# Moving an 18 KB weight load from SyncE's queue to ScalarE's queue in a grouped 1x1 convolution

## The chip, the cores and the metric

The kernel runs on 1 core of one Trainium2 chip. The metric is the device time of one execution in microseconds (us), lower is better. Each run also has a span, from the first to the last instruction or transfer that the profiler records; it is some 2 us shorter than the time.

## The reference

```
x: (1, 512, 512, 192) bf16      w: (1, 1, 4, 48, 48) bf16
xg  = x.reshape(1, 512, 512, 4, 48)
out = einsum('bhwgc,gcd->bhwgd', xg, w[0, 0])     # k = 1, no padding
```

Each of 262,144 pixels has 192 channels in 4 groups of 48, and each group is multiplied by its own 48x48 matrix. The input and the output are 100.7 MB each; the weights are 18 KB.

## The kernel before

Pixels are cut into pieces. The input loads go out of SyncE's queue into a ring of 5 slots in SBUF (104 pixels a partition each). TensorE (PE) transposes a pair of pixel groups against an identity, VectorE (DVE) copies the transposes out of PSUM, PE multiplies with the weights, ScalarE (ACT) writes the result back into the same ring columns, and the stores go out of ScalarE's queue. The first slot is cut into pieces of 8, 20, 32 (and then whole slots of 104) so that PE can start early.

The weights come in as `w_sb`, 48 partitions with four rows of 96 bytes each. PE spreads them with a selection matrix `esel` to blocks in PSUM, and DVE copies those to `wt`, which the product matmuls read. On PE this building of the weights stands ahead of the first transposes.

```
        @block.sync
        def _(sp):
            wq = Waiter(sp)
            sp.dma_start(w_sb[:], wv).then_inc(w_sem, 16)
            for p in pieces:
                for q in pieces:
                    if q.slot == p.slot - RCOLS // BIG:
                        wq.wait(st_sem[q.i], st_val[q])        # the slot's stores have landed
                for dram, sbuf in transfers(xf, ring, p):
                    sp.dma_start(sbuf, dram).then_inc(ld_sem[p.i], 16)

        # tensor (cut)
            build_weights()                # waits for e_sem (esel) and w_sem (w_sb)
            wq.wait(id_sem, 1)
            transposes(0)                  # waits for ld_sem of the first piece
            wq.wait(wc_sem, 1)             # wt copied by DVE
            for pair in range(NP):
                if pair + 1 < NP:
                    transposes(pair + 1)
                matmuls(pair)

        @block.scalar
        def _(act):
            wq = Waiter(act)
            todo = list(stores)
            # ... (cut) per group: wait for mm_done, act.copy of o_ps into the ring, then its stores
```

## Time and profile before

| | before |
|---|---|
| time, median of 3 runs | 485.05 us (484.9 to 485.07) |
| span of the profiled run | 483.3 us |
| busy PE / ACT / DVE | 89% / 81% / 52% |
| DMA, mean over the span | 418 GB/s |
| packet time of the two big DMA queues over 16 engines | 470.8 us |

The first view is the page's row of 40 equal slices: the mean busy share of the 16 DMA engines in tenths (9 is 90% or more), and what they moved.

```profile
DMA  8999999999999999999999999999999999999993
GB/s 351 431 406 421 449 425 421 422 424 442 434 428 419 425 420 439 425 434 424 431 434 437 424 431 428 432 431 426 434 428 428 430 424 422 439 416 427 429 390 156
```

The engines are full in every slice but the first and the last. Next, stretches of the span: length, busy time of each engine, granted PE clock, DMA share and GB/s (the last two numbers).

```profile
1.00:2.00 1.00, 0.00 (x0) 0.00 (x0) 0.00 (x0) 1.00 (x1) 0.91 (x4) 1.00 0.10 10
2.00:3.00 1.00, 0.34 (x9) 0.37 (x10) 0.00 (x0) 0.08 (x1) 0.00 (x0) 1.00 0.62 110
3.00:4.00 1.00, 0.22 (x6) 0.08 (x3) 0.66 (x1) 0.00 (x0) 0.00 (x0) 1.00 1.03 370
60.00:455.00 395.00, 376.00 (x5527) 341.70 (x5526) 220.75 (x231) 345.63 (x461) 0.00 (x0) 0.99 1.00 429
...
474.00:476.00 2.00, 0.00 (x0) 0.00 (x0) 0.00 (x0) 0.00 (x0) 0.00 (x0) 0.50 0.58 244
478.00:480.00 2.00, 0.00 (x0) 0.00 (x0) 0.00 (x0) 0.00 (x0) 0.00 (x0) 0.50 0.16 66
```

The middle runs at a share of 1.00; the first 3 us and the last 15 us do not. In the tail only stores are left, and at 478 us a share of 0.16 means that two or three of the 16 engines still work. So the time is the start of the stream, plus a full stream, plus the lag of the last engine.

The start in the timeline (start, length, engine, line, operation; SPq and ACTq are the issues on SyncE's and ScalarE's queues):

```profile
0.80 1.28 ACT L260 ACT_TABLE_LOAD   x1 [0.80 <-PEq L280]
0.80 0.38 SPq L169 DMA_DIRECT2D w_sb<-in_w_dram  x1
...
1.24 3.47 SPq L175 DMA_DIRECT2D ring<-in_x_dram  x7
...
2.66 0.56 PE L188 MATMUL o_ps<-w_sb,esel 48*128 48x48 bf16 x10 [2.66 <-DMA w_sb<-in_w_dram]
...
4.68 1.44 PE L203 MATMUL xT_ps<-ident,ring 128*128 128x128 bf16 x12 [1.47 <-DMA ring<-in_x_dram]
...
7.02 1.44 PE L203 MATMUL xT_ps<-ident,ring 128*128 128x128 bf16 x12 [0.89 <-DMA ring<-in_x_dram]
```

The weight issue takes SyncE's queue from 0.80 to 1.24 us, and the seven input loads that need no ring space follow. The weights land early (PE starts on them at 2.66 us), and PE waits for each of the first input loads.

The chain of waits, followed back from the last instruction, has one long piece at its start:

```profile
2.65 21.79 DMA ring<-in_x_dram
```

Until 24.4 us the chain is a load that PE waits for, not PE's own work. After that it runs mostly through PE; its summary by line:

```profile
by line: PE o_ps L218 31.5%; PE xT_ps L203 22.2%; DMA ring<-in_x_dram 20.3%; DMA out_dram<-ring 18.9%; ACT ring L260 1.2%; issue 0.8%; SPq L175 0.3%; ACTq L254 0.2%; SPq L169 0.1%
```

So PE (54% of the chain) is a rival to the DMA engines (39%) for what sets the pace.

### The profile page before, as it was taken

To read this page: it belongs to the slowest core of one execution; us is meant where nothing else is said; L and a number is where in the kernel's file an instruction comes from. 1 tells how busy PE (TensorE), PEld (TensorE's weight loads), DVE (VectorE), ACT (ScalarE), POOL (GpSimd) and SP (SyncE) were. 2 spreads that over 40 slices of the span, in tenths; PEclk is the share of its full clock that TensorE was granted. 3 is DMA by queue.
4 is the path that set the end of the run, shared out by engine and by line. 5 is a ranking of instruction groups with operands and counts; after the bars stand their busy time and mean duration, and the time that the engine had idled before them with its cause. 6 is when DMAs were issued, how large, how long until landed. Compare 5 with 4: busy or idle time off the path is not lost.

```text
span 483.3 us, 13933 instructions
## 1 busy us (share of the span) xinstructions
PE 431.3 (89%) x6262; PEld 392.1 (81%) x6262; DVE 250.2 (52%) x262; ACT 392.6 (81%) x522; POOL 1.3 (0%) x8
## 2 busy tenths in 40 slices
PE   5699999999999999998599999979998999999910
PEld 5599888898898889887588988969787898899800
DVE  2345655656555565564256555544554655556500
ACT  2669999999999999998299999877888999999920
POOL 1000000000000000000000000000000000000000
PEclk9979999999999999999799999998999999999965
DMA  8999999999999999999999999999999999999993
GB/s 351 431 406 421 449 425 421 422 424 442 434 428 419 425 420 439 425 434 424 431 434 437 424 431 428 432 431 426 434 428 428 430 424 422 439 416 427 429 390 156
DMA packets 7834, 202.23 MB, mean 418 GB/s; under 512 B 1056, under 2 KB 1056, under 8 KB 1696
## 3 DMA queue, kind: packets, MB, share of 16 engines
q10 hardware_dynamic: 4360, 100.67, 48.7%
q1 hardware_dynamic: 3416, 100.68, 48.7%
q8 instruction: 50, 0.82, 0.6%
q14 instruction: 8, 0.07, 0.0%
HBM read 100.68 MB, written 100.66 MB: 417 GB/s over the span
## 4 chain that ended last, share of the span: by engine, by line
PE 54%; DMA 39%; ACT 1%; issue 1%; SPq 0%; ACTq 0%
PE o_ps L218 31%; PE xT_ps L203 22%; DMA ring<-in_x_dram 20%; DMA out_dram<-ring 19%; ACT ring L260 1%; SPq L175 0%; ACTq L254 0%; SPq L169 0%
## 5 line engine op out<-in xcount | busy, mean ns | idle before, releaser
L260 ACT CAST ring<-o_ps 128x768 bf16<-128x768 f32 x521 | 391.3, 802 | 68.5 <-PE o_ps L218 61.0
L242 DVE COPY xT_sb<-xT_ps 128x1536 bf16<-128x1536 bf16 (+1 forms) x261 | 249.6, 956 | 206.0 <-PE xT_ps L203 206.0
L218 PE MATMUL o_ps<-wt,xT_sb 128*128 128x144 bf16 (+1 forms) x3126 | 292.0, 236 | 5.9 <-ACT ring L260 1.3
L218 PEld LDWEIGHTS o_ps<-wt,xT_sb 128*128 128x128 bf16 x3126 | 212.0, 99 | 43.4 <-ACT ring L260 30.2
L203 PE MATMUL xT_ps<-ident,ring 128*128 128x128 bf16 x3126 | 222.7, 221 | 21.1 <-DMA ring<-in_x_dram 21.1
L203 PEld LDWEIGHTS xT_ps<-ident,ring 128*128 128x128 bf16 x3126 | 191.1, 99 | 22.7 <-DMA ring<-in_x_dram 19.8
L188 PE MATMUL o_ps<-w_sb,esel 48*128 48x48 bf16 x10 | 0.6, 210 | 2.7 <-DMA w_sb<-in_w_dram 2.7
L188 PEld LDWEIGHTS o_ps<-w_sb,esel 48*128 48x128 bf16 x10 | 0.5, 113 | 2.6 <-POOL esel L158 2.6
L236 DVE CAST wt<-o_ps 128x480 bf16<-128x480 f32 x1 | 0.7, 658 | 3.3 <-PE o_ps L188 3.3
L260 ACT ACT_TABLE_LOAD x1 | 1.3, 1283 | 0.8 <-PEq L280 0.8
L158 POOL TENSOR_SCALAR_AFFINE_SELECT esel<-esel 48x272 bf16<-48x272 bf16 x1 | 0.4, 405 | 0.0
L155 POOL MEMSET esel<- 48x272 bf16 x1 | 0.3, 318 | 0.3 <-POOLq L280 0.3
L162 POOL TENSOR_SCALAR_AFFINE_SELECT ident<-ident 128x128 bf16<-128x128 bf16 x1 | 0.3, 285 | 0.0
L156 POOL MEMSET ident<- 128x128 bf16 x1 | 0.2, 198 | 0.0
L280 POOL MEMSET const-bfloat16-1.0<- 128x1 bf16 x1 | 0.1, 102 | 0.0
L280 POOL MEMSET const-uint8-127<- 128x1 uint8 x1 | 0.1, 102 | 0.0
L280 POOL MEMSET const-float32-0.0<- 128x1 f32 x1 | 0.1, 98 | 0.3 <-issue 0.3
L280 POOL MEMSET const-float32-1.0<- 128x1 f32 x1 | 0.1, 98 | 0.0
## 6 DMA issues: line engine op xcount, KB each, us to landing
ring<-in_x_dram SPq DMA_DIRECT2D x19, 4992.0 KB, 37.5
out_dram<-ring ACTq DMA_DIRECT2D x13, 4992.0 KB, 45.5
out_dram<-ring ACTq DMA_DIRECT2D x10, 2496.0 KB, 47.7
out_dram<-ring ACTq DMA_DIRECT2D x3, 1536.0 KB, 19.7
ring<-in_x_dram SPq DMA_DIRECT2D x1, 1536.0 KB, 8.4
out_dram<-ring ACTq DMA_DIRECT2D x1, 1152.0 KB, 16.6
ring<-in_x_dram SPq DMA_DIRECT2D x1, 960.0 KB, 5.2
out_dram<-ring ACTq DMA_DIRECT2D x1, 960.0 KB, 28.6
```

Of the source, the lines that this page charges most:

```text
L155: gp.memset(esel[:], 1.0).then_inc(p0_sem, 1)
L156: gp.memset(ident[:], 1.0).then_inc(p1_sem, 1)
L158: gp.affine_select(out=esel[:], in_=esel[:], pattern=[[-1, ECOLS]], compare_op=AluOpType.is_equal, fill=0.0, base=ESHIFT, channel_multipli ...
L162: gp.affine_select(out=ident[:], in_=ident[:], pattern=[[-1, 128]], compare_op=AluOpType.is_equal, fill=0.0, base=0, channel_multiplier=1) ...
L188: last = pe.matmul(o_ps[:, NOB - 1, col:col + CG], lhsT=esel[:, s0:s0 + 128], rhs=w_sb[:, g, :], start=True, stop=True, skip_group_check=True)
L203: last = pe.transpose(xT_ps[:, g % NXP, j * 128:(j + 1) * 128], xg[:, j * 128:(j + 1) * 128], ident[:])
L218: last = pe.matmul(o_ps[:, v % NOB, c0_:c1_], lhsT=xs[:, j * 128:(j + 1) * 128], rhs=wt[:, WOFF[tc]:WOFF[tc] + (c1_ - c0_)], start=(tc == ...
L236: dve.tensor_copy(wt[:], o_ps[:, NOB - 1, 0:WCOLS]).then_inc(wc_sem, 1)
L242: dve.tensor_copy(xT_sb[pair % NXS][:, 0:n * 2 * UC].rearrange("p (g c) -> p g c", g=n), xT_ps[:, b0:b0 + n, 0:2 * UC]).then_inc(e_done, 1)
L260: act.copy(dst, o_ps[:, v % NOB:v % NOB + 2, 0:UC]).then_inc(fa_done, 1)
L280: nc = _bacc.Bacc("TRN2", target_bir_lowering=False, num_devices=1)
```

## The change

Its intent: the first instruction of SyncE's queue should be the first input load, so that the long stream of loads starts one issue time earlier. ACT has nothing to do then but its table load.

```diff
         @block.sync
         def _(sp):
             wq = Waiter(sp)
-            sp.dma_start(w_sb[:], wv).then_inc(w_sem, 16)
             for p in pieces:
@@
         @block.scalar
         def _(act):
             wq = Waiter(act)
+            act.dma_start(w_sb[:], wv).then_inc(w_sem, 16)
             todo = list(stores)
```

## The prediction

> **What bounds the kernel now.** The DMA engines. The page's slice row reads 9 tenths or more in all slices but the first and the last, 418 GB/s mean, and the stretch view has a share of 1.00 from 20 to 400 us. Summed from the packet records, the two big queues hold 470.8 us of work for each of the 16 engines, in a span of 483.3 us. PE (89%) and ACT (81%) are near, but PE stands idle 21 us for loads. Unused are the head (first packet at 1.79 us) and the tail (share 0.80 at 466 us, 0.08 at 480 us: a few engines finish last).
>
> **What the change removes.** The timeline shows the weight load first in SyncE's queue: issued at 0.80 us, 0.38 us long, the first input load at 1.24 us. In the packet records the weight's 192 packets of 96 bytes run from 1.79 to 2.19 us, about 0.01 us each, and the first input packet starts at 2.31 us. Issue to first packet takes 1.0 to 1.07 us. Without the weight ahead, the first input load goes out at 0.80 us, its packets start near 1.85 us: 0.44 us earlier, like the six loads behind it.
>
> **What it adds.** One issue of 0.4 us on ScalarE's queue: free, for ACT first works (but for its table load) at 9.29 us. It may fall on either side of the table load (0.80 to 2.08 us). The Trainium skill ("ScalarE: Activation LUTs", What ACT_TABLE_LOAD costs) gives 1283 ns for that load, and the trace agrees (1283 ns). If the issue stands before it, the weight lands near 2.5 to 3 us; if after, at 2.1 + 1.7 = 3.8 us, or up to 5 us because its small packets then take turns with 3072-byte ones of 0.12 us (an estimate: 12 packets per engine, each behind one of those). The Trainium skill ("DMA: Bandwidth & Descriptors", Issuing engines are not separate DMA queues) says that both queues run on the same 16 engines, so no bandwidth is gained, only issue time.
>
> **What is on the critical path.** The weights build (0.56 us on PE) precedes the first transposes, which now begin at 4.68 us, when the first input load lands. Early weight: they begin near 4.25 us. Late weight: at 5.0 to 5.6 us. PE waits for loads again at 7.0 us and, in the chain of waits, until 24.5 us (a DMA piece of 21.8 us), so a late start is absorbed. What counts is when the saturated DMA stream starts: 0.44 us earlier, less some 0.12 us per engine for the weight's packets, which formerly ran on idle engines. So 0.3 to 0.45 us off 485.05, under 0.1%.
>
> **Prediction.** 484.7 us, range 484.2 to 485.3; within 2% with 98%.
>
> **What the profile would show.** The first input load issued at 0.80 us in SyncE's queue; its first packet near 1.85 us; a weight issue in ScalarE's queue at 0.80 or about 2.1 us; the weight's wait on PE longer than 2.7 us if it is the latter; the second block of transposes near 6.6 us (7.02 now); from there all about 0.4 us earlier; total packet time unchanged.
>
> **What would make it wrong.** The order in which loads and stores meet at the DMA engines could change the lag of the last engine by more than the 0.44 us. Two queues issuing together could slow each other. A very late weight would delay the first stores.

## The result and the profile after

A ratio is the mean time of one kernel's fast runs over that of the other's of the same rounds, so it is not quite the ratio of the medians quoted.

| | before | after |
|---|---|---|
| time, median of 6 runs each | 485.03 us (484.9 to 485.07) | 484.85 us (484.62 to 486.0) |
| ratio | | 1.0001 (95%: 0.9988 to 1.0013) |
| span of the profiled run | 483.3 us | 482.9 us |
| first large input packet starts | 2.31 us | 1.80 us |
| weight's packets of 96 bytes run | 1.79 to 2.20 us | 2.60 to 3.74 us |
| weight: issue to landing | 1.7 us | 3.5 us |
| packet time of the two big queues over 16 engines | 470.8 us | 470.3 us |

The two packet rows and the last row come from the trace's record of every DMA packet. Five of the six times after lie at 484.6 to 485.3 us; one is 486.0 us, with a span of 484.0 us, and it alone makes the ratio 1.0001. That first comparison could not say whether anything was won.

The slices after:

```profile
DMA  8999999999999999999999999999999999999993
GB/s 352 450 418 400 446 422 421 429 451 423 425 426 431 442 420 427 424 437 441 425 421 432 429 438 423 435 425 433 435 418 441 417 426 428 428 426 426 427 387 143
```

The same stretches:

```profile
1.00:2.00 1.00, 0.00 (x0) 0.00 (x0) 0.00 (x0) 0.76 (x1) 0.91 (x4) 1.00 0.24 34
2.00:3.00 1.00, 0.00 (x0) 0.00 (x0) 0.00 (x0) 0.53 (x1) 0.00 (x0) 1.00 0.70 212
3.00:4.00 1.00, 0.00 (x0) 0.00 (x0) 0.00 (x0) 0.00 (x0) 0.00 (x0) 1.00 1.10 404
60.00:455.00 395.00, 375.10 (x5512) 341.18 (x5510) 220.10 (x230) 344.45 (x460) 0.00 (x0) 0.99 1.00 429
...
474.00:476.00 2.00, 0.00 (x0) 0.00 (x0) 0.00 (x0) 0.00 (x0) 0.00 (x0) 0.50 0.41 174
478.00:480.00 2.00, 0.00 (x0) 0.00 (x0) 0.00 (x0) 0.00 (x0) 0.00 (x0) 0.50 0.15 61
```

More moves between 1 and 4 us (34, 212, 404 GB/s, against 10, 110, 370: together 0.16 MB, or 0.37 us at 429 GB/s), the middle is the same, and the tail ends a little sooner. The start of the timeline:

```profile
0.80 0.41 ACTq L247 DMA_DIRECT2D w_sb<-in_w_dram  x1
0.80 3.29 SPq L174 DMA_DIRECT2D ring<-in_x_dram  x7
...
1.24 1.28 ACT L260 ACT_TABLE_LOAD   x1 [1.24 <-PEq L280]
...
4.39 0.56 PE L187 MATMUL o_ps<-w_sb,esel 48*128 48x48 bf16 x10 [4.39 <-DMA w_sb<-in_w_dram]
4.88 1.20 PEld L202 LDWEIGHTS xT_ps<-ident,ring 128*128 128x128 bf16 x12
4.88 1.46 PE L202 MATMUL xT_ps<-ident,ring 128*128 128x128 bf16 x12
...
6.57 1.44 PE L202 MATMUL xT_ps<-ident,ring 128*128 128x128 bf16 x12 [0.23 <-DMA ring<-in_x_dram]
```

Both queues issue at 0.80 us. The weight's issue stands before the table load. PE now gets its weights at 4.39 us in place of 2.66 us, so the first transposes start 0.20 us later than before (4.88 against 4.68), but the second ones start 0.45 us earlier (6.57 against 7.02), because they wait for an input load that lands earlier. The chain begins accordingly:

```profile
2.17 21.63 DMA ring<-in_x_dram
```

### The profile page after: what moved, and what is told of

It is laid out like the page before. It is cut to its first block, busy times and chain, and to the rows that moved or that the text cites. A ratio compares the mean times of both kernels' runs of the same rounds, so it can differ in the third digit from the quotient of the medians.

```text
span 482.9 us, 13933 instructions
## 1 busy us (share of the span) xinstructions
PE 429.5 (89%) x6262; PEld 390.6 (81%) x6262; DVE 250.1 (52%) x262; ACT 392.5 (81%) x522; POOL 1.3 (0%) x8
## 4 chain that ended last, share of the span: by engine, by line
PE 54%; DMA 39%; ACT 1%; issue 1%; SPq 0%; ACTq 0%
PE o_ps L217 31%; PE xT_ps L202 22%; DMA ring<-in_x_dram 20%; DMA out_dram<-ring 19%; ACT ring L260 1%; SPq L174 0%; ACTq L254 0%
```

## The experiments

Twelve runs of ten kernels were made in three sets of five rounds against the kernel before (the record gives another chip number for each set); all were correct. The changed kernel itself is in the first two sets only. In the first set the kernel before is slower than in the first comparison (median 485.43 against 485.03 us), so the absolute times expected for ahead4 and act_and_copy are missed by 0.4 and 0.1 us; what counts is the difference to the kernel before. Theory A: the end shifts one for one with the start of the saturated stream. Rival B: the end is set by the last engine's own lag, which a shift of the start does not reach. Theories C and D (the second queue's packets disturb the loads; a late weight holds PE back) were added for what could take a gain back. "Span difference" is the mean span of the kernel's fast runs minus that of the kernel before in the same rounds; the plus-minus is one standard error, worked out from the spread of the two.

| run | first large packet, us | weight landed, us (profiled run) | median time (before in the same rounds), us | span difference, us |
|---|---|---|---|---|
| after_again | 1.80 | 4.4 | 484.69 (485.43) | -0.55 +- 0.08 |
| after_third | 1.81 | 4.4 | 484.77 (485.26) | -0.44 +- 0.05 |
| ahead4 | 4.23 | 2.8 | 487.32 (485.43) | +1.87 +- 0.10 |
| act_and_copy | 2.29 | 3.0 | 485.34 (485.43) | -0.03 +- 0.09 |
| p0_on_act | 1.89 | 4.2 | 484.75 (485.19) | -0.44 +- 0.06 |
| w_third | 1.81 | 7.1 | 485.0 (485.19) | -0.44 +- 0.07 |
| w_second | 1.80 | 4.3 | 485.47 (485.43) | -0.03 +- 0.19 |
| w_second_again | 1.79 | 4.2 | 485.53 (485.26) | +0.02 +- 0.14 |
| copy_second | 1.81 | 4.4 | 485.24 (485.19) | +0.22 +- 0.34 |
| p1_on_act | 1.79 | 19.5 | 485.39 (485.26) | +0.18 +- 0.09 |
| w_after_p0 | 1.81 | 22.2 | 485.44 (485.19) | +0.20 +- 0.09 |
| w_after_p1 | 1.81 | 28.1 | 488.4 (485.26) | +3.12 +- 0.11 |

### The changed kernel again, twice (no edit)

> The changed kernel once more, in the same rounds as the others. Theory A (the end of the kernel shifts one for one with the start of the saturated stream of input loads; that start is 0.51 us earlier than before, 1.80 against 2.31 us): median 484.4 to 484.7 us against 485.0 before, ratio 0.9988 to 0.9995. Rival B (the end is set by the last DMA engine's own lag, which a shift of the start does not reach or which varies by more): the ratio's interval contains 1 and single runs spread by over 0.5 us.

> The changed kernel a third time, so that its gain and its spread rest on more runs. So far its spans are 482.7 to 483.2 us with one of 484.0 (11 runs), those of the kernel before 483.1 to 483.6 in the same rounds. Theory A: the median span is 0.4 to 0.6 us shorter than that of the kernel before of these rounds. Theory B: no clear difference.

Measured: ratios 0.9985 (0.9972 to 0.9999) and 0.9988 (0.9976 to 1.0001). All ten spans lie at 482.7 to 482.9 us; the 18 spans of the kernel before in these rounds lie at 483.1 to 483.6. The spans do not overlap, which decides it, for the second interval still contains 1. So there is a gain, of 0.44 to 0.55 us (0.1%). In the first comparison the one run of 486.0 us hid it. Why that run was longer was not found; it is not profiled.

### More copies of the weight load ahead

```diff
             sp.dma_start(w_sb[:], wv).then_inc(w_sem, 16)
+            for k in range(4):
+                sp.dma_start(w_x[:, k, :, :], wv).then_inc(x_sem, 16)
             for p in pieces:
```

(`w_x` is a scratch tile; SyncE waits for `x_sem` after its last load.)

> The kernel before with four more copies of the weight load (to a scratch tile, 18 KB each) in SyncE's queue ahead of the first input load, which goes out near 3.0 us in place of 1.24 us. Theory A: 1.76 us longer than before, 486.6 to 486.9 us. Theory B: under half of that, 485.0 to 485.9 us.

Measured: the first large packet starts at 4.23 us in place of 2.31, which is 1.92 us later; the span is 1.87 us longer. The changed kernel starts 0.51 us earlier and is 0.44 to 0.55 us shorter. The end follows the start one for one in both directions: theory A holds, and rival B, which allowed under half of it, falls.

### The other queue without the earlier start

```diff
   # on the changed kernel
         def _(sp):
             wq = Waiter(sp)
+            for k in range(1):
+                sp.dma_start(w_x[:, k, :, :], wv).then_inc(x_sem, 16)
             for p in pieces:
```

> The changed kernel (weight in ScalarE's queue) with one copy of the weight load put first in SyncE's queue, so that the first input load goes out near 1.24 us as before. It has the other queue but not the earlier start. Theory A: 484.9 to 485.2 us, as before. If the gain comes from the other queue in itself, and not from the earlier start: 484.5 to 484.8 us. Theory C: the spread is narrow, as before, if the weight's packets now pass ahead of the loads; its landing is then near 1.7 us after its issue in place of 3.5 us.

Measured: no gain (-0.03 us). The weight is in ScalarE's queue as in the changed kernel, the first input load goes out at 1.25 us as before. So the other queue is worth nothing in itself. The weight landed 2.0 us after its issue, since its packets (1.79 us and after) now passed ahead of the loads.

### The mirror image: the first input load on ScalarE's queue

```diff
   # on the kernel before: the weight stays first in SyncE's queue
-                for dram, sbuf in transfers(xf, ring, p):
+                for dram, sbuf in transfers(xf, ring, p) if p.i != 0 else ():
                     sp.dma_start(sbuf, dram).then_inc(ld_sem[p.i], 16)
@@
         def _(act):
             wq = Waiter(act)
+            for dram, sbuf in transfers(xf, ring, pieces[0]):
+                act.dma_start(sbuf, dram).then_inc(ld_sem[0], 16)
```

> The mirror image of the change: the weight stays first in SyncE's queue (0.80 us), and the first input load goes out of ScalarE's queue at 0.80 us; the second and later input loads out of SyncE's queue at 1.24 us and after, all as in the changed kernel. Theory A' (what counts is when all input loads go out, whichever queue does it): median span 0.4 to 0.6 us shorter than before, as the changed kernel. If the queue that carries the weight matters: no gain, 0.2 us or less.

Measured: -0.44 us, the changed kernel's gain, with spans of 482.8 and 482.9 us only. It does not matter which queue carries the weight; it matters that two queues issue at 0.80 us and the loads therefore go out one issue earlier.

### The weight second or third in SyncE's queue

```diff
   # on the kernel before, its own first line taken out; w_second (w_third has p.i == 1)
                 for dram, sbuf in transfers(xf, ring, p):
                     sp.dma_start(sbuf, dram).then_inc(ld_sem[p.i], 16)
+                if p.i == 0:
+                    sp.dma_start(w_sb[:], wv).then_inc(w_sem, 16)
```

> The weight load stays in SyncE's queue, but as its second instruction, behind the first input load. The first input load is issued at 0.80 us as in the changed kernel, the second one 0.44 us later than there. Theory A: 484.5 to 484.8 us, because the engines have the first load's 384 KB to move (about 0.9 us) while the weight is issued, so the stream starts early and does not run dry. Theory C (what widened the spread and took back part of the gain is the second queue's weight packets taking turns with the loads at the start): this kernel has a spread as narrow as before, under 0.2 us, and the full 0.4 to 0.5 us of gain. Theory B: 485.0, spread unlike either.

> The weight second in SyncE's queue, once more. Its first five spans fell at 482.9 and 483.0 or at 483.5 to 483.7 us. If its missing gain was chance: median span within 0.2 us of the changed kernel's. If it is real (all loads but the first are issued at the same time as before, so only 384 KB move earlier): median span 0.3 to 0.6 us above the changed kernel's, as at first.

> The weight third in SyncE's queue, behind the second input load. Two input loads (1.34 MB, over 3 us of work at full rate) are 0.44 us early, the other five as before. Plain theory A (the stream never runs dry, so later issue times do not matter): median span 0.4 to 0.6 us shorter than before. Theory A' (every one of the first loads must go out early): 0.2 us or less. The weight lands near 6.5 to 7 us, which should cost nothing, as PE's start at 20 us cost 0.2 us or so in the run with the second load in ScalarE's queue.

Measured: w_third has the full gain (-0.44 us, five spans of 482.8 to 483.0) on one queue alone. (By the medians of the times it is 0.19 us; the times scatter more than the spans.) Only the first two input loads (384 and 960 KB) are early there, and PE gets its weights at 7.1 us; neither takes anything away. w_second gains nothing in either set (-0.03, +0.02 us), though its first large packet starts at 1.80 us too. Its spans are scattered: 482.9 and 483.0 next to 483.5 and 483.7 in the first set. That was a miss for plain theory A.

### A copy of the weight load between the first two input loads

```diff
   # on the changed kernel
                 for dram, sbuf in transfers(xf, ring, p):
                     sp.dma_start(sbuf, dram).then_inc(ld_sem[p.i], 16)
+                if p.i == 0:
+                    sp.dma_start(w_x[:, 0, :, :], wv).then_inc(x_sem, 16)
```

> The changed kernel (weight in ScalarE's queue at 0.80 us, first input load at 0.80 us) with a copy of the weight load put between the first and the second input load in SyncE's queue, so that all input loads have the issue times of the kernel with the weight second. If those issue times are why that one gained nothing: no gain here either, 0.2 us or less against before. If it was the weight itself behind the first input load in the same ring: the changed kernel's gain, 0.4 to 0.6 us.

Measured: no clear gain; the spans are 483.0 to 483.4 us and one of 485.2 (the profiled one), and without that one the mean is 0.12 us under before. So it is not the weight, and not its landing, that spoils w_second. What the two kernels share is a small load between the first and the second input load and, with it, an issue of the second load that is 0.44 us later than in the changed kernel; these two were not separated. In the profiled runs the second input load's packets of 7680 bytes end late:

| run | last packet of 7680 bytes ends | first packet of the third load starts |
|---|---|---|
| before | 6.55 us | 6.13 us |
| after / after_again / after_third | 6.04 / 6.92 / 6.04 us | 5.77 / 5.54 / 5.73 us |
| w_third / p0_on_act | 6.32 / 6.49 us | 5.57 / 5.66 us |
| w_second / w_second_again | 6.74 / 8.73 us | 5.71 / 5.73 us |
| copy_second | 8.13 us | 5.87 us |

In w_second_again some engines are on the third load 3.0 us before the last one has finished the second; in copy_second 2.3 us. The timeline of w_second_again shows PE waiting for that load until 9.19 us, in place of 6.57 us in the changed kernel:

```profile
0.80 0.37 SPq L174 DMA_DIRECT2D ring<-in_x_dram  x1
0.80 1.28 ACT L261 ACT_TABLE_LOAD   x1 [0.80 <-PEq L281]
...
1.23 0.41 SPq L176 DMA_DIRECT2D w_sb<-in_w_dram  x1
...
1.68 4.50 SPq L174 DMA_DIRECT2D ring<-in_x_dram  x6
...
9.19 1.44 PE L204 MATMUL xT_ps<-ident,ring 128*128 128x128 bf16 x12 [3.01 <-DMA ring<-in_x_dram]
```

The lag alone does not tell a lost gain from a kept one: after_again had 1.4 us and kept its gain. In the profiled runs the number of packets in flight does. Counted from the packet records between 4.0 and 5.0 us, its mean is 16.2 in the kernel before, the changed kernel (all three profiled runs), act_and_copy, p0_on_act, w_third, and also in the profiled run of w_second, whose span of 482.9 us is as short as the changed kernel's. (It is a little over 16 because records of following packets overlap slightly.) In w_second_again (span 483.7 us) it is 14.2, from 3.5 to 5.25 us, and in copy_second (485.2 us) 14.5. So in those profiled runs of the two kernels that won nothing, about two of the 16 engines stood idle while the second load was due. That this costs the 0.5 us is likely but rests on one profiled run each; it does not explain the 485.2 us. The records do not say which engine a packet ran on, and why a small load in that place, or the later issue, leaves engines idle in some runs stays open.

### The weight load held back

```diff
   # on the changed kernel; w_after_p1 (w_after_p0 waits for ld_sem[0])
         def _(act):
             wq = Waiter(act)
+            act.wait_ge(ld_sem[1], 16)
             act.dma_start(w_sb[:], wv).then_inc(w_sem, 16)
```

> The changed kernel, with ScalarE waiting for the second input load to land (about 6.5 us) before it issues the weight load. The weight lands some 5 us later than in the changed kernel, near 9 to 10 us, and PE's whole start moves back by as much; no byte and no input load moves. Theory A (PE has slack at the start, only the start of the stream counts): span as the changed kernel's, within 0.2 us. Theory D (a late weight takes back part of the gain, since PE starts later): 1 us or more longer.

> The changed kernel, with ScalarE waiting for the first input load to land (near 4 us) before it issues the weight load. Its 12 packets per engine then take turns with packets of 7680, 12288 and at last 39936 bytes: landing between 9 and 20 us (with the weight issued at 6.4 us it took 21.6 us). Theory A (PE has slack at the start, here up to 15 us or so): median span within 0.3 us of the changed kernel's 482.8. Theory D (PE has little slack): 1 us or more longer.

Measured: w_after_p1 is 3.12 us longer than before, w_after_p0 0.20 us longer. The first number seems to contradict theory A, until one looks at when the weight landed. I had expected 9 to 10 us. The chain of waits of w_after_p1 has:

```profile
1.25 5.16 DMA ring<-in_x_dram
6.42 21.57 DMA w_sb<-in_w_dram
28.69 2.67 PE xT_ps L202 x24
```

The 18 KB took 21.6 us from issue to landing, against 1.7 us in the kernel before. The packet records show most of the cause: its 192 packets ran from 10.79 to 26.07 us in eleven bunches 1.48 us apart (16 packets each, one of 32), and the loads' packets of 39,936 bytes take 1.476 us each (median). The Trainium skill ("DMA: Bandwidth & Descriptors", Queues, rings and completion order) says that an engine takes turns between the queues that have work, a packet at a time; that agrees. A bunch of 16 fits one packet for each of the 16 engines, so each packet of 96 bytes (0.012 us) waited for a whole packet of the other queue. (The rest of the 21.6 us: the first bunch came 4.4 us after the issue, which was not explained, and the landing 1.9 us after the last packet.) In the changed kernel the same turns were taken with packets of 3072 bytes (0.121 us each), 2.60 to 3.74 us in all. So a landing at 28 us costs 3.6 us more than the changed kernel; one at 22 us costs 0.64 to 0.75 us (0.20 + 0.44 or 0.55); one at 7.1 us (w_third) costs nothing. PE's slack at the start is large, but it has an end, and the page of w_after_p1 shows a part of it, in the sixth slice (60.8 to 72.9 us):

```profile
GB/s 348 442 454 398 408 336 420 416 433 438 427 422 445 427 429 420 431 436 427 425 438 427 408 427 433 429 433 422 433 432 429 422 437 414 446 412 428 427 413 149
```

336 GB/s stand there in place of 425 in the kernel before. From 64.5 to 66.2 us only 2.5 packets are in flight on average, by the packet records: the first seven loads have landed, the eighth, which needs a slot whose stores have landed, is issued at 66.6 us (59.5 in the changed kernel), and the fourth store at 65.4 us (49.6). From 60 to 70 us the 16 engines lose about 1.6 us each in this way; the rest of the 3.6 us was not traced.

w_after_p0 has no such gap, and it decides whether PE or the DMA stream sets the pace. Its PE starts late:

```profile
22.24 0.56 PE L187 MATMUL o_ps<-w_sb,esel 48*128 48x48 bf16 x10 [22.24 <-DMA w_sb<-in_w_dram]
```

Its first transposes start 18 us later than in the kernel before (22.73 against 4.68 us), its ninth store is still issued 9.5 us later (167.0 against 157.5 us), its last 0.3 us later (462.2 against 461.9 us), and the mean span is 0.20 us longer. If PE's own pace set the end, most of the 18 us would have stayed. So PE, though it is most of the chain, has slack, and the DMA stream sets the end.

As to what was expected: w_after_p1 met the number of theory D, but on a landing far later than assumed; w_after_p0, sent with the landing known, fell between the two (0.64 to 0.75 us over the changed kernel, against at most 0.3 or at least 1).

### Two input loads at 0.80 us

```diff
   # on the changed kernel: SyncE leaves out the second input load
+            for dram, sbuf in transfers(xf, ring, pieces[1]):
+                act.dma_start(sbuf, dram).then_inc(ld_sem[1], 16)
             act.dma_start(w_sb[:], wv).then_inc(w_sem, 16)
```

> The second input load is issued by ScalarE's queue at 0.80 us, at the same time as the first by SyncE's queue, and the weight after it on ScalarE's queue (1.24 us). The other input loads come out of SyncE's queue 0.44 us earlier. If what holds the stream back at 2 to 3 us (212 GB/s) is that too few loads are issued: span up to 0.4 us shorter than the changed kernel's. If it is the DMA engines' own start: the same within 0.2 us.

Measured: 0.18 us longer than before, so 0.6 us worse than the changed kernel. It does not answer the question that it was made for, because it moved the weight as well. Issued at 1.24 us, only 0.44 us later than in the changed kernel, behind 128 larger packets of its own queue, the weight met the large packets (7.19 to 17.40 us) and landed 18.2 us after its issue:

```profile
1.24 18.18 DMA w_sb<-in_w_dram
20.10 2.62 PE xT_ps L202 x24
```

How much of the 0.6 us is PE's late start was not separated from other effects, such as the later start of the stores.

No experiment pointed to a version that beats the changed kernel; w_third and p0_on_act equal it in the span.

## Why the prediction was right

- **Size.** 484.7 us was predicted, in 484.2 to 485.3; measured were medians of 484.85, 484.69 and 484.77 us. The gain was put at 0.3 to 0.45 us. By the spans it is 0.44 to 0.55 us, by the times 0.5 to 0.7 us in the two later sets. The first set did not resolve it. The range says little by itself: it also holds 485.03 us, the time before, so a change without any effect would have met it too. What speaks for the prediction is the mechanism below, shown by the later runs.
- **The stream bounds the kernel, and its start shifts the end one for one.** Right for these kernels: -0.51 us of start gave -0.44 and -0.55, +1.92 us gave +1.87. An early first packet alone is not enough, though: w_second and copy_second have it and gain nothing.
- **The start moves by 0.44 us.** A little small. The first large packet moved from 2.31 to 1.80 us, 0.51 us. The 1.07 us from issue to first packet was not constant: it was 1.00 us for the first load of SyncE's queue.
- **0.12 us per engine taken back by the weight's packets.** No run shows it; p0_on_act and w_third, which move the same packets, gain the same 0.44 us.
- **The second queue adds no bandwidth; only issue time is saved.** Right: act_and_copy has the second queue and no gain, w_third has one queue and the gain.
- **When the weight lands.** The prediction left open on which side of the table load the issue falls, and it falls before it. For that case I wrote 2.5 to 3 us, and that was wrong: PE got it at 4.39 us. The estimate of packets that take turns with 0.12 us ones was made for the other case only; it holds for this one.
- **A late start of PE is absorbed.** Right for 4.4 and 7.1 us. It ends somewhere before 22 us.
- **The second block of transposes near 6.6 us.** 6.57 us in the profiled run (6.60 and 7.38 in the two repeats).

## What to carry to other kernels

When the DMA engines are full from the first load to the last store, one issue taken off the front of the load queue is worth about its issue time, here 0.44 to 0.55 us of 485 for an issue of 0.44 us, and it does not matter which of the two queues carries the small load. Here, though, the first two big loads had to follow each other directly: with a small load between them nothing was won, with one behind them (w_third) the whole gain. A small load of many short packets should go out ahead of the big loads or beside small ones: beside packets of 40 KB each of its packets waits for a whole one, and 18 KB took 18 to 22 us. A gain of 0.1% is seen only with many runs of both kernels in the same rounds; here the first six runs could not show it.

## What the Trainium skill lacked or had wrong

- "DMA: Bandwidth & Descriptors", Queues, rings and completion order: it describes turns packet by packet, but not what they do to a small load beside large ones. In these runs 18 KB in 96-byte packets landed 1.7 us after issue with nothing beside it, 3.5 us beside packets of 3072 bytes, and 18.0 to 21.6 us where it met packets of 39,936 bytes (1.48 us from one bunch of its packets to the next).
- The same page, Issuing engines are not separate DMA queues: it says that issuing from several engines saves only the sequencer's issue time. The runs agree for the gain (0.44 to 0.55 us for an issue of about 0.4 us). It does not say that moving a small load to a second queue can delay it by more than that (landing 3.5 in place of 1.7 us after issue).
- The same page, Latency and other measured facts: it has about 600 ns to the first byte for loads issued from SyncE or ScalarE. Here, for the first transfers of a run, 0.98 to 1.09 us passed from the start of the issue to the start of the first packet, of which the issue itself took 0.38 to 0.42 us; the two figures agree if the page counts from the end of the issue, which it does not say. Behind or beside other loads it was longer: 1.8 us for the weight in the changed kernel, 4.4 us in w_after_p1.
- No page has what w_second and copy_second showed: an 18 KB load between the first two input loads took away the 0.5 us that an early start gave. In the two profiled runs of these kernels without the gain about two of the 16 engines stood idle near 4.5 us (14.2 and 14.5 packets in flight in place of 16.2); why is open.
